# Two edits to the start of a fused attention and two-layer MoE kernel: an issue order on TensorE, and a third staging buffer for weights

## The chip, the core and the metric

The kernel runs on one core of a Trainium2 chip. Its five engines each work through a queue of their own in order: TensorE (PE in the profile; its weight loads are PEld), VectorE (DVE), ScalarE (ACT), GpSimd (POOL) and SyncE (SP), which here issues most of the DMAs. The metric is the device time of one execution in microseconds (us), as the median of several runs; lower is better. One further execution was taken with the hardware profiler, and all rows below come from that one.

## What is computed

Decay attention on 4 batches of 8 heads, sequence 576 and head size 64, then two dense feed-forward layers on the 2304 tokens. Inputs are float32 but for the weights, which are float64.

```python
scores = q @ k.T / 8 + (cum[:, None] - cum[None, :])   # cum = cumsum(log(clip(f))), causal
x = softmax(scores) @ v            # tokens x 512
h = x @ w_in ; g = maximum(0.01 * h, h) ; y = g @ w_out     # first MoE, width 2048
out = ((y @ w_a) * (y @ w_b)) @ w_o2                        # second MoE, width 1536
```

## The kernel before

**Precision.** A matmul operand is split into a high and a low part (`_hi`, `_lo`), and a product is three matmuls (hi·hi, hi·lo, lo·hi) into one accumulator. Weights arrive as pairs of 32-bit words of a float64. `load_weight` loads one piece of 128 x 512 of them by one DMA of 512 KB into a tile `raw`, and `from_double` builds the float32 in a tile `c`: on ACT an absolute value (L94); on DVE a clamp (L95), a shift (L96), and two merges that read `raw` (L97, L100). `split` then writes the high part on ACT (L87) and the low part on DVE (L88). So a piece costs two instructions on ACT and five on DVE. `raw` and `c` have two buffers each in the pool `stage`; a `raw` buffer is free once L100 has read it.

**First MoE.** Tokens are worked in chunks of 256. For a chunk i and a pair pr of weight column blocks, `l1` makes a group `h_i_pr` of 24 matmuls of 128 x 256 (L574), ACT writes `gh` and `hs`, DVE writes `gl` (L586), and `l2` adds 24 matmuls into `y_i_0` and `y_i_1` (L601). Eight pairs make a chunk. The weights stay in SBUF for all chunks, so chunk 0 is the one that waits for loading and conversion: pair pr needs the pieces `wi_2pr`, `wi_2pr+1`, `wo_2pr`, `wo_2pr+1`.

**Attention.** A block is a batch b and a half r of its rows. Block (0,0) fills chunk 0 of x, block (0,1) fills chunk 1 and a part of chunk 2. Per head there are scores `s` (and `s4` for the last 64 rows), a reduction on DVE (`p`, L320 and L361), an exponential on ACT, transposes `pp`, products with v (`av`), and per pair of heads a division `xn` on DVE and a transpose `px`, whose result ACT and DVE split into `xh` and `xl` of the chunk. Batch 0 works in plain float32; there each score or `av` matmul of the program is two in the trace.

**What sets the order.** The kernel is written in a framework that lists instructions by priority, times them with a planner's model of the engines, and so fixes each engine's queue when the program is built. The code calls block (0,0) with weight loads in between, then with raised priority the first two pairs of chunk 0, then block (0,1) with loads and further pairs, then the rest. The queue of PE starts a matmul only after all those ahead of it, and so do DVE, ACT and SP with theirs.

Of the kernel before, what the change touches and what calls it, by code (L numbers as in the profile page):

```python
# [17 lines left out]
P = 128  # L18
# [8 lines left out]
def kernel(  # L27
# [13 lines left out]
    nc = tc.nc  # L41
    B, H, S, D = q.shape
# [4 lines left out]
    NF1, NF2, ND = F1 // P, F2 // P, DM // P  # L47
# [57 lines left out]
    def load_weight(pool, stg_pool, src, name, W, RB, **kw):  # L105

        hi = pool.tile([P, 512], F32R, tag="w", name=f"{name}_hi", **kw)
        lo = pool.tile([P, 512], F32R, tag="w", name=f"{name}_lo", **kw)
        for z in range(0, 512, W):
            raw = stg_pool.tile([P, W, 2], I32, tag="raw", bufs=RB, name=f"raw_{name}_{z}")  # L110
            view = raw.rearrange("p n t -> p (n t)")
            if len(src.shape) == 3:
                view = view.rearrange("p (a b) -> p a b", b=2 * P)
                nc.sync.dma_start(view, src[:, z // P : (z + W) // P, :])
            else:
                nc.sync.dma_start(view, src[:, 2 * z : 2 * (z + W)])
            c = stg_pool.tile([P, W], I32, tag="t", bufs=2, name=f"c_{name}_{z}")
            split(hi[:, z : z + W], lo[:, z : z + W], from_double(raw, c), nc.vector)
        return hi, lo

# [9 lines left out]
    mp = moe_ctx.enter_context(tc.tile_pool(name="moe_a", bufs=2, side="right"))  # L130
    stage_ctx = ExitStack()
    stage = stage_ctx.enter_context(tc.tile_pool(name="stage", bufs=2, side="right"))
    late = {}
    ps_y = moe_ctx.enter_context(tc.tile_pool(name="ps_y", bufs=2, space=PSUM))
    att_ctx = ExitStack()
    ap_ = att_ctx.enter_context(tc.tile_pool(name="att", bufs=1))
    ps_a = att_ctx.enter_context(tc.tile_pool(name="ps_att", bufs=1, space=PSUM, side="right"))


# [1 line left out]
    nc.sync.dma_start(fs, f.rearrange("b h s -> (b h) s"))  # L141
    nc.vector.tensor_scalar(fs, fs, 0.0001, 1.0, op0=ALU.max, op1=ALU.min)
    nc.scalar.activation(fs, fs, AF.Ln)
    ones = ap_.tile([B * H, S], F32, tag="tk", name="ones")
    nc.vector.memset(ones, 1.0)
    cum = ap_.tile([B * H, S], F32, tag="cumb", bufs=3, name="cum")
    nc.vector.tensor_tensor_scan(cum, ones, fs, 0.0, op0=ALU.mult, op1=ALU.add)
# [22 lines left out]
    def att_scores(b, r, h, st):  # L170
# [56 lines left out]
        else:  # L227
# [3 lines left out]
            for u in range(2):  # L231
                for e in range(2):
# [2 lines left out]
                    nc.sync.dma_start(dst[:, lead // 32 : nqc, :], src[:, : nqc - lead // 32, :])  # L235
                    if lead:
                        nc.sync.dma_start(dst[:, 0:2, :], src[:, nqc - 2 :, :])
            tq = ap_.tile([P, 320], F32, tag="tq", name=f"tq_{nm}")
            dve_att.transpose(out=tq[:, :nq], in_=xq[:, :nqc, :].rearrange("p c d -> p (c d)"))

            qhh = ap_.tile([P, 384], F32R, tag="qhh", bufs=2, name=f"qhh_{nm}")
            qll = ap_.tile([P, 384], F32R, tag="qll", bufs=2, name=f"qll_{nm}")
            lasts[h] = qhh, qll
            z0 = 64 if r == 1 and j == 1 else 0
            if r == 1:
# [8 lines left out]
            if j == 0:  # L254
                xk = ap_.tile([P, 18, 32], F32, tag="xk", name=f"xk_{nm}")
                for u in range(2):
                    for e in range(2):
                        nc.sync.dma_start(
                            xk[u * 64 + e * 32 : u * 64 + e * 32 + 32, :nkc, :],
                            k[b, h + u, 0:nk, e * 32 : e * 32 + 32].rearrange("(c i) d -> i c d", i=32),  # L260
                        )
                tk = ap_.tile([P, S], F32, tag="tk", name=f"tk_{nm}")
                dve_att.transpose(out=tk[:, :nk], in_=xk[:, :nkc, :].rearrange("p c d -> p (c d)"))
                qks[pair] = tk

# [291 lines left out]
    def load_a(fi):  # L557
# [2 lines left out]
            *load_weight(wpool, stage, rows(w_out, fi), f"wo_{fi}", 512, 2, bufs=4 * NF1),  # L560
        )

    def l1(i, pr):
        ch, cl = x_chunk(i)
        last = i >= NB1 - 2
        hps = (pools["ps_ab"] if last else ps_y).tile(
            [P, 2, T1], F32, tag="ab0" if last else "h", bufs=2 if last else 1, name=f"h_{i}_{pr}"
        )
        for u in range(2):
            wih, wil = wa[2 * pr + u][0], wa[2 * pr + u][1]  # L570
            n = 0
            for c in reversed(range(ND)):
                for w, x in ((wih, ch), (wih, cl), (wil, ch)):
                    nc.tensor.matmul(  # L574
                        hps[:, u, :], w[:, c * P : c * P + P], x[:, c, :], start=(n == 0), stop=(n == 3 * ND - 1)
                    )
                    n += 1

        hs = mp.tile([P, 2, T1], F32, tag="hs", name=f"hs_{i}_{pr}")
        gh = mp.tile([P, 2, T1], F32R, tag="gh", name=f"gh_{i}_{pr}")  # L580
        gl = mp.tile([P, 2, T1], F32R, tag="gl", name=f"gl_{i}_{pr}")
        with tc.high_priority(offset=1):
            nc.scalar.activation(gh, hps, AF.Prelu, alpha=0.01)
# [103 lines left out]
    def att_steps(n):  # L687

        if n == 0:

            sts = [{} for _ in range(H)]
            scores = [att_scores(*blocks[n], h, sts[h]) for h in range(H)]
            values = [att_values(*blocks[n], h, sts[h]) for h in range(H)]
            before = None
            for h in range(0, 2):
                next(scores[h])
            for h in range(0, H, 2):
                for z, _ in enumerate(beside(beside(*scores[h : h + 2]), before)):
                    if z == 3:
                        for g in scores[h + 2 : h + 4]:  # L700
                            next(g)
                    yield
                before = chain(*values[h : h + 2])
            yield from before
            return
        second = None
        for h in range(H):
            st = {}
            yield from beside(att_scores(*blocks[n], h, st), second)
            second = att_values(*blocks[n], h, st)  # L710
# [22 lines left out]
    def work(i, fi):  # L733
        pend.append((i, fi, *l1(i, fi)))
        if len(pend) > 1:
            l2(*pend.pop(0))
# [5 lines left out]
    def load_next():  # L742
        nonlocal loaded
        if loaded < NF1:
            load_a(loaded)
            loaded += 1
# [7 lines left out]
        load_next()  # L754
    with tc.high_priority(offset=2000):
        work(*zero.pop(0))
        work(*zero.pop(0))
    for s, _ in enumerate(att_steps(1)):
        if s % 8 == 7:
            load_next()  # L760
        if s % 16 == 15 and 2 * (NF1 // 2 - len(zero)) + 2 <= loaded:
            work(*zero.pop(0))
    while zero:
        load_next()
        load_next()
# [1 line left out]
    for item in one[:4]:  # L767
        work(*item)
    stage_ctx.close()
    late["p"] = moe_ctx.enter_context(tc.tile_pool(name="late", bufs=1, side="right"))  # L770
    att_tail(0)
    for _ in att_steps(2):
# [73 lines left out]
```

## Time and profile before

| | us |
|---|---|
| median of 3 runs (lowest, highest) | 1111.56 (1110.79, 1111.98) |
| the profiled execution's own time | 1109.59 |
| its span, first to last instruction | 1107.8 |
| PE busy in the span | 1079.2 (97%) |
| DVE busy | 614.0 (55%) |
| ACT busy | 543.2 (49%) |

The shares of busy time are means over very different stages: on the page's 40 slices DVE is 7 to 8 tenths busy until about the middle and 1 to 2 tenths in the last third, while PE shows 9 nearly throughout. A PE that counts as busy isn't one that runs at its peak, since ends of matmuls are modelled; for PE the distance between starts is the better measure.

### The profile page before, as it was taken

To read this page: it belongs to the slowest core of one execution; us is meant where nothing else is said; L and a number is where in the kernel's file an instruction comes from. 1 tells how busy PE (TensorE), PEld (TensorE's weight loads), DVE (VectorE), ACT (ScalarE), POOL (GpSimd) and SP (SyncE) were. 2 spreads that over 40 slices of the span, in tenths; PEclk is the share of its full clock that TensorE was granted. 3 is DMA by queue.
4 is the path that set the end of the run, shared out by engine and by line. 5 is a ranking of instruction groups with operands and counts; after the bars stand their busy time and mean duration, and the time that the engine had idled before them with its cause. 6 is when DMAs were issued, how large, how long until landed. Compare 5 with 4: busy or idle time off the path is not lost.

```text
span 1107.8 us, 19615 instructions
## 1 busy us (share of the span) xinstructions
PE 1079.2 (97%) x7021; PEld 967.2 (87%) x7021; DVE 614.0 (55%) x1484; ACT 543.2 (49%) x1257; POOL 204.5 (18%) x434
## 2 busy tenths in 40 slices
PE   5899999999999999999999999999999999999998
PEld 3577779999999999999999997888888888888897
DVE  5869887887777777677478877412111211211122
ACT  4656668878787878768554454312111211211121
POOL 4423322434243432333000000102001000100000
PEclk9879999999999999999999999999999999999999
DMA  7645545442452334422054454202000100100010
GB/s 196 195 130 172 159 120 103 96 94 48 79 124 62 94 58 83 109 62 53 9 165 144 142 152 152 76 1 76 1 1 20 48 1 1 48 1 1 1 39 20
DMA packets 185729, 86.77 MB, mean 78 GB/s; under 512 B 143840, under 2 KB 173536, under 8 KB 185632
## 3 DMA queue, kind: packets, MB, share of 16 engines
q1 hardware_dynamic: 180736, 80.80, 28.6%
q10 hardware_dynamic: 4896, 4.72, 1.3%
q8 instruction: 56, 0.92, 0.4%
q14 instruction: 41, 0.34, 0.1%
HBM read 75.96 MB, written 9.51 MB: 77 GB/s over the span
## 4 chain that ended last, share of the span: by engine, by line
PE 72%; DMA 11%; DVE 8%; ACT 4%; issue 3%; SPq 1%; POOL 0%; ACTq 0%; DVEq 0%; POOLq 0%
PE ab L653 25%; PE o L676 13%; PE h L574 11%; PE y L601 10%; PE s L76 5%; PE av L76 5%; PE pp L76 3%; DMA raw_wa<-in_moe_w_a_dram 3%; DMA raw_wb<-in_moe_w_b_dram 2%; DMA raw_wc<-in_moe_w_out_dram 1%; DMA xq<-in_q_dram 1%; DMA cumb<-cum_dram 1%; DMA raw_wi<-in_moe_w_in_dram 1%; DMA raw_wo<-in_moe_w_out_dram 1%; DMA sy<-y_dram 1%
## 5 line engine op out<-in xcount | busy, mean ns | idle before, releaser
L659 DVE TENSOR_TENSOR p<-ab,p 128x512 f32<-128x512 f32 (+1 forms) x60 | 38.3, 638 | 274.6 <-PE ab L653 272.0
L574 PE MATMUL h<-xh,wi_hi 128*128 128x256 f32 x576 | 164.6, 286 | 1.2 <-ACT wi_hi L87 1.2
L574 PE MATMUL h<-xh,wi_lo 128*128 128x256 f32 x576 | 164.1, 285 | 0.9 <-DVE wi_lo L88 0.9
L574 PE MATMUL h<-xl,wi_hi 128*128 128x256 f32 x576 | 164.3, 285 | 0.0
L601 PE MATMUL y<-gl,wo_hi 128*128 128x256 f32 x576 | 161.7, 282 | 1.0 <-DVE gl L586 1.0
L601 PE MATMUL y<-gh,wo_lo 128*128 128x256 f32 x576 | 161.1, 282 | 0.0
L601 PE MATMUL y<-gh,wo_hi 128*128 128x256 f32 x576 | 159.4, 282 | 0.0
L658 ACT COPY p<-ab 128x512 f32<-128x512 f32 (+1 forms) x60 | 32.7, 544 | 169.1 <-PE ab L653 168.7
L574 PEld LDWEIGHTS h<-xh,wi_hi 128*128 128x128 f32 x576 | 109.8, 191 | 5.2 <-issue 2.3
L574 PEld LDWEIGHTS h<-xh,wi_lo 128*128 128x128 f32 x576 | 109.8, 191 | 2.5 <-DVE wi_lo L88 1.1
L601 PEld LDWEIGHTS y<-gl,wo_hi 128*128 128x128 f32 x576 | 108.4, 188 | 2.9 <-DVE gl L586 1.6
L574 PEld LDWEIGHTS h<-xl,wi_hi 128*128 128x128 f32 x576 | 109.8, 191 | 0.8 <-issue 0.4
L601 PEld LDWEIGHTS y<-gh,wo_lo 128*128 128x128 f32 x576 | 108.3, 188 | 1.7 <-issue 1.2
L601 PEld LDWEIGHTS y<-gh,wo_hi 128*128 128x128 f32 x576 | 107.3, 188 | 1.8 <-issue 0.8
L313 POOL TENSOR_SCALAR p<-cumb,ncum_t 128x384 f32<-128x384 f32 (+1 forms) x112 | 75.1, 678 | 162.4 <-PE pp L76 47.8
L87 ACT CAST pph<-p 128x512 fp32r<-128x512 f32 (+1 forms) x60 | 34.8, 580 | 126.3 <-DVE p L659 126.2
L291 ACT ACTIVATE p<-p,stat 128x384 f32<-128x384 f32 (+4 forms) x128 | 77.0, 603 | 34.5 <-DVE stat L320 27.2
L88 POOL TENSOR_TENSOR yl<-sy,yh 128x512 fp32r<-128x512 f32 (+1 forms) x16 | 19.2, 1211 | 393.7 <-ACT yh L87 393.6
L653 PE MATMUL ab<-yh,wb_hi 128*128 128x512 f32 (+1 forms) x240 | 88.3, 368 | 0.9 <-DVE p L659 0.6
L653 PE MATMUL ab<-yh,wa_hi 128*128 128x512 f32 (+1 forms) x240 | 88.1, 367 | 0.0
L653 PE MATMUL ab<-yh,wa_lo 128*128 128x512 f32 (+1 forms) x240 | 88.1, 367 | 0.0
L653 PE MATMUL ab<-yl,wa_hi 128*128 128x512 f32 (+1 forms) x240 | 88.1, 367 | 0.0
(168 smaller groups left out, 2612.6 us busy)
## 6 DMA issues: line engine op xcount, KB each, us to landing
cumb<-cum_dram SPq DMA_DIRECT2D x32, 288.0 KB, 3.9
raw_wi<-in_moe_w_in_dram SPq DMA_DIRECT2D x16, 512.0 KB, 4.0
raw_wo<-in_moe_w_out_dram SPq DMA_DIRECT2D x16, 512.0 KB, 4.0
raw_wa<-in_moe_w_a_dram SPq DMA_DIRECT2D x12, 512.0 KB, 3.5
raw_wb<-in_moe_w_b_dram SPq DMA_DIRECT2D x12, 512.0 KB, 3.5
raw_wc<-in_moe_w_out_dram SPq DMA_DIRECT2D x12, 512.0 KB, 3.6
xq<-in_q_dram SPq DMA_DIRECT2D x144, 32.0 KB, 2.0
y_dram<-yo ACTq DMA_DIRECT2D x18, 256.0 KB, 3.0
```

What stands on the lines that cost most here:

```text
L76: return method(*args, **kw)
L87: nc.scalar.copy(hi, src)
L88: (lo_engine or nc.gpsimd).tensor_tensor(out=lo, in0=src, in1=f32(hi), op=ALU.subtract)
L291: act_att.activation(pt, pt, AF.Exp, bias=stat[:, 0, s : s + 1], scale=-1.0, accum_out=stat[:, 1, s : s + 1])
L313: pool_att.tensor_scalar(pt, cumb[:, :n], 1.0, ncum_t[:, t, bh : bh + 1], op0=ALU.mult, op1=ALU.add)
L574: nc.tensor.matmul(hps[:, u, :], w[:, c * P : c * P + P], x[:, c, :], start=(n == 0), stop=(n == 3 * ND - 1))
L601: nc.tensor.matmul(o, w[:, d * P : d * P + P], g[:, u, :], start=(fi == 0 and n == 0 and d % 2 == 0), stop=(fi == NF1 - 1 and n == 2 and d ...
L653: nc.tensor.matmul(o[:, :tn], w[:, c * P : c * P + P], y[:, c, :tn], start=(m == 0), stop=(m == 3 * ND - 1))
L658: nc.scalar.copy(p[:, :tn], ab[0][:, :tn])
L659: nc.vector.tensor_tensor(out=p[:, :tn], in0=ab[1][:, :tn], in1=p[:, :tn], op=ALU.mult)
L676: nc.tensor.matmul(o, g[:, t * P : t * P + P], w, start=(fi == 0 and m == 0), stop=(fi == NF2 - 1 and m == 2))
```

## The change

Two edits. The first records the last of the 24 matmuls of `h_0_0` and wraps the calls for block (0,1) in `issue_after`, which adds an edge from that matmul to every PE instruction that the block traces: in PE's queue they come behind it, without a wait for its end. It holds for PE alone. The second makes a pool `more` with one buffer of `raw` and one of `c`; every third piece (number 2, 5, 8 and so on, in the order of the calls) uses it. To make room, the tiles `tq`, `qll` and `tk` of batches 1 to 3 move to a pool `att_b` that is opened in the place of `more` once the weights of the first MoE are converted, and `ones` shares another tag.

```diff
         for z in range(0, 512, W):
-            raw = stg_pool.tile([P, W, 2], I32, tag="raw", bufs=RB, name=f"raw_{name}_{z}")
+            third = "more" in late and piece[0] % 3 == 2
+            piece[0] += 1
+            words, bufs = (late["more"], 1) if third else (stg_pool, RB)
+            raw = words.tile([P, W, 2], I32, tag="raw", bufs=bufs, name=f"raw_{name}_{z}")
...
-            c = stg_pool.tile([P, W], I32, tag="t", bufs=2, name=f"c_{name}_{z}")
+            c = words.tile([P, W], I32, tag="t", bufs=1 if third else 2, name=f"c_{name}_{z}")
...
+    more_ctx = att_ctx.enter_context(ExitStack())
+    late["more"] = more_ctx.enter_context(tc.tile_pool(name="more", bufs=1))
...
-    ones = ap_.tile([B * H, S], F32, tag="tk", name="ones")
+    ones = ap_.tile([B * H, S], F32, tag="p4", name="ones")
...
-            tq = ap_.tile([P, 320], F32, tag="tq", name=f"tq_{nm}")
+            tq = late["att"].tile([P, 320], F32, tag="tq", name=f"tq_{nm}")
...
-                    nc.tensor.matmul(
+                    end[0] = nc.tensor.matmul(
...
         work(*zero.pop(0))
+        first_end = end[0]
         work(*zero.pop(0))
-    for s, _ in enumerate(att_steps(1)):
-        if s % 8 == 7:
-            load_next()
-        if s % 16 == 15 and 2 * (NF1 // 2 - len(zero)) + 2 <= loaded:
-            work(*zero.pop(0))
+    with tc.issue_after(first_end.ins if hasattr(first_end, "ins") else first_end):
+        for s, _ in enumerate(att_steps(1)):
+            if s % 8 == 7:
+                load_next()
+            if s % 16 == 15 and 2 * (NF1 // 2 - len(zero)) + 2 <= loaded:
+                work(*zero.pop(0))
...
     stage_ctx.close()
+    more_ctx.close()
+    del late["more"]
+    late["att"] = more_ctx.enter_context(tc.tile_pool(name="att_b", bufs=1))
```

The planner then lays out all queues anew. On PE, just ahead of the first product of the first MoE, this stood before (`tk`, `tq`, `s`, `s4` and `pp` with 0_1 in the name belong to block (0,1), `px_0_0_7` is the last transpose of block (0,0)):

```order
L76 MATMUL av_0_0_7_580<-vn_0_0_6_562,ph_0_0_7_571 128x64 x3
L76 MATMUL s_0_1_0_2_741<-kn_0_1_0_709,qn_0_1_0_708 128x384
L76 MATMUL s_0_1_0_3_750<-kn_0_1_0_709,qn_0_1_0_708 128x512
L76 MATMUL px_0_0_7_614<-ident_65,xn_0_0_7_587 128x128 x2
L76 MATMUL s4_0_1_0_0_760<-kn_0_1_0_709,qn_0_1_0_708 64x288
L76 MATMUL pp_0_1_0_0_807<-ident_65,p_0_1_0_2_736 128x128 x3
L76 MATMUL s4_0_1_0_1_763<-kn_0_1_0_709,qn_0_1_0_708 64x288
L76 MATMUL pp_0_1_0_1_813<-ident_65,p_0_1_0_3_745 128x128 x4
L76 MATMUL tq_0_1_2_935<-ident_65,xq_0_1_2_925 128x128 x2
L76 MATMUL tq_0_1_2_935<-ident_65,xk_0_1_2_926 128x64
L76 MATMUL tk_0_1_2_0_940<-ident_65,xk_0_1_2_926 128x128 x2
L76 MATMUL s_0_1_1_2_803<-kn_0_1_0_709,qn_0_1_0_708 128x384
```

and now:

```order
L76 MATMUL px_0_0_5_560<-ident_65,xn_0_0_5_532 128x128 x2
L76 MATMUL av_0_0_7_583<-vn_0_0_6_565,ph_0_0_6_568 128x64 x3
L76 MATMUL av_0_0_7_583<-vn_0_0_6_565,ph_0_0_7_574 128x64 x3
L76 MATMUL px_0_0_7_617<-ident_65,xn_0_0_7_590 128x128 x2
L581 MATMUL h_0_0_622<-xh_0_312,wi_0_hi_188 128x256
```

All of block (0,1), the ten rows of it shown before and the eight transposes `tq_0_1_0` and `tk_0_1_0` that stood some rows higher, has gone behind the 24 products; `h_0_0` follows `px_0_0_7`.

On DVE, ahead of the last `xl_0`, which makes chunk 0 of x complete, this stood before (`c_wo_4`, `c_wi_5` are weight pieces under conversion):

```order
L76 TENSOR_TENSOR xn_0_0_7_587<-av_0_0_7_580,rec_0_0_7_577 128x2x64 x2
L100 SCALAR_TENSOR_TENSOR c_wo_4_0_489<-raw_wo_4_0_487,c_wo_4_0_489 128x512
L320 ISA p_0_1_0_2_736,stat_0_1_0_707<-s_0_1_0_2_741,p_0_1_0_2_736 128x384
L320 ISA stat_0_1_0_707 128x1
L95 TENSOR_SCALAR c_wi_5_0_536<-c_wi_5_0_536 128x512
L320 ISA p_0_1_0_3_745,stat_0_1_0_707<-s_0_1_0_3_750,p_0_1_0_3_745 128x512
L320 ISA stat_0_1_0_707 128x1
L88 TENSOR_TENSOR wo_4_lo_486<-c_wo_4_0_489,wo_4_hi_485 128x512
L96 TENSOR_SCALAR c_wi_5_0_536<-c_wi_5_0_536 128x512
L361 ISA p4_0_1_0_754,st4_0_1_0_755<-s4_0_1_0_0_760,p4_0_1_0_754 64x288
L361 ISA st4_0_1_0_755 64x1
L76 TENSOR_TENSOR xl_0_310<-px_0_0_7_614,xh_0_309 128x256
```

and now:

```order
L88 TENSOR_TENSOR wo_5_lo_548<-c_wo_5_0_551,wo_5_hi_547 128x512
L76 TENSOR_TENSOR xn_0_0_7_590<-av_0_0_7_583,rec_0_0_7_580 128x2x64 x2
L100 SCALAR_TENSOR_TENSOR c_wi_6_0_597<-raw_wi_6_0_595,c_wi_6_0_597 128x512
L95 TENSOR_SCALAR c_wo_6_0_609<-c_wo_6_0_609 128x512
L96 TENSOR_SCALAR c_wo_6_0_609<-c_wo_6_0_609 128x512
L95 TENSOR_SCALAR c_wi_7_0_775<-c_wi_7_0_775 128x512
L97 SCALAR_TENSOR_TENSOR c_wo_6_0_609<-raw_wo_6_0_607,c_wo_6_0_609 128x512
L88 TENSOR_TENSOR wi_6_lo_594<-c_wi_6_0_597,wi_6_hi_593 128x512
L96 TENSOR_SCALAR c_wi_7_0_775<-c_wi_7_0_775 128x512
L76 TENSOR_TENSOR xl_0_313<-px_0_0_7_617,xh_0_312 128x256
```

The conversions run further ahead: the piece in work at that point was `wi_5` and is `wi_7` now, and the three reductions of block (0,1) have gone behind.

On PE, ahead of `px_0_1_7`, the last transpose that chunk 1 of x waits for, stood before (`h_0_7` is the last product group of chunk 0, and nine more of its matmuls follow these rows; the `s_1_0` are first scores of batch 1):

```order
L76 MATMUL s_1_0_1_0_2252<-ks_1_0_1_2236,qhh_1_0_1_2232 128x128
L76 MATMUL s_1_0_1_0_2252<-ks_1_0_1_2236,qll_1_0_1_2233 128x128
L574 MATMUL h_0_7_1820<-xh_0_309,wi_15_hi_1601 128x256
L574 MATMUL h_0_7_1820<-xl_0_310,wi_15_hi_1601 128x256
L76 MATMUL s_1_0_1_1_2270<-ks_1_0_1_2236,qhh_1_0_1_2232 128x256
L76 MATMUL s_1_0_1_1_2270<-ks_1_0_1_2236,qll_1_0_1_2233 128x256
L574 MATMUL h_0_7_1820<-xh_0_309,wi_15_lo_1602 128x256
```

and now:

```order
L76 MATMUL av_0_1_7_1893<-vn_0_1_6_1772,ph_0_1_7_1878 128x64 x4
L76 MATMUL s_1_0_1_1_2277<-ks_1_0_1_2243,qhh_1_0_1_2239 128x256
L76 MATMUL s_1_0_1_1_2277<-ks_1_0_1_2243,qll_1_0_1_2240 128x256
L76 MATMUL s_1_0_2_0_2324<-ks_1_0_2_2314,qhh_1_0_2_2303 128x128
L76 MATMUL s_1_0_2_0_2324<-ks_1_0_2_2314,qll_1_0_2_2304 128x128
L76 MATMUL px_0_1_7_1911<-ident_65,xn_0_1_7_1908 128x128 x2
```

Chunk 0, with its last products and the last conversions, now stands well ahead of the last heads of block (0,1); before, `h_0_7` stood directly ahead of `px_0_1_7`. At the first matmul of `h_1_1` both queues have issued the same PE instructions, and from there on they differ only by small exchanges.

## Rows read from the trace of the kernel before

**Rows 1.** Busy time in windows: stretch, us, busy (instructions) by engine, PEclk, DMA share, GB/s.

```profile
13.40:58.40 45.00, 35.71 (x135) 24.39 (x135) 35.19 (x104) 27.57 (x73) 21.77 (x46) 0.87 0.74 201
62.78:175.16 112.38, 109.29 (x730) 89.72 (x730) 94.60 (x235) 70.38 (x164) 31.61 (x48) 0.96 0.51 138
153.69:167.09 13.40, 11.15 (x79) 10.63 (x78) 12.47 (x43) 9.18 (x25) 1.14 (x4) 0.87 0.35 84
180.00:300.00 120.00, 119.86 (x1000) 118.26 (x999) 94.67 (x275) 97.06 (x254) 45.27 (x107) 1.00 0.41 83
```

**Rows 2.** Waits of DVE from 13.4 to 58.4 us: total us, times, longest.

```profile
DVE c_wi L95 <- ACT c_wi L94: 5.3, 5, 2.3
...
DVE c_wo L95 <- ACT c_wo L94: 1.0, 1, 1.0
```

**Rows 3.** Waits of DVE from 58.4 to 77.5 us.

```profile
DVE p L320 <- PE s L76: 5.7, 2, 2.9
```

**Rows 4.** Waits of DVE from 77.5 to 167.4 us.

```profile
DVE c_wi L95 <- ACT c_wi L94: 3.3, 3, 2.2
```

**Rows 5.** Timeline: start, us, instruction (last use of raw_wo_4; last xl_0; c_wo_5).

```profile
53.42 0.69 DVE L100 SCALAR_TENSOR_TENSOR c_wo<-raw_wo,c_wo 128x512 int32<-128x512 int32 x1
...
57.97 0.41 DVE L76 TENSOR_TENSOR xl<-px,xh 128x256 fp32r<-128x256 f32 x1
...
61.03 0.66 ACT L94 ACTIVATE c_wo<-raw_wo 128x512 f32<-128x512 f32 x1
```

**Rows 6.** Lines of DVE, 77.5 to 167.4: count | busy us, mean ns | idle.

```profile
L88 DVE TENSOR_TENSOR wi_lo<-c_wi,wi_hi 128x512 fp32r<-128x512 f32 x10 | 7.2, 724 | 0.2
L100 DVE SCALAR_TENSOR_TENSOR c_wo<-raw_wo,c_wo 128x512 int32<-128x512 int32 x10 | 7.0, 698 | 0.2
...
L96 DVE TENSOR_SCALAR c_wo<-c_wo 128x512 int32<-128x512 int32 x10 | 4.4, 439 | 0.1
```

**Rows 7.** DMA issues of the page: count, KB each, median us to landing.

```profile
raw_wi<-in_moe_w_in_dram SPq DMA_DIRECT2D x16, 512.0 KB, 4.0
```

**Rows 8.** Lines of PE by form, 62.78 to 175.16 (six of 24 groups).

```profile
L574 PE MATMUL h<-xh,wi_hi 128*128 128x256 f32 x72 | 22.3, 310 | 1.2 <-ACT wi_hi L87 1.2
...
L601 PE MATMUL y<-gl,wo_hi 128*128 128x256 f32 x64 | 18.2, 287 | 0.0
...
L76 PE MATMUL av<-vn,ph 128*128 128x64 f32 x112 | 13.9, 274 | 0.0
L76 PE MATMUL pp<-ident,p 128*128 128x128 f32 x68 | 11.4, 287 | 0.4 <-DVE xl L374 0.4
L76 PE MATMUL s<-kn,qn 64*128 64x512 f32 x14 | 7.9, 641 | 0.4 <-DVE stat L361 0.4
...
L76 PE MATMUL tq<-ident,xk 64*128 64x64 f32 x2 | 0.5, 273 | 0.0
```

**Rows 9.** The chain that ended last: start, us, piece (seven pieces without a wait).

```profile
62.85 5.05 PE h L574 x24
...
119.62 1.11 PE av L76 x10
120.73 0.44 PE pp L76 x4
121.17 0.84 PE s L76 x2
...
122.72 1.05 PE s L76 x2
...
126.29 0.68 PE s L76 x2
...
548.59 2.80 PE h L574 x24
```

**Rows 10.** Windows around the first product, columns as in the first group.

```profile
44.00:62.78 18.78, 17.89 (x64) 10.88 (x63) 13.92 (x36) 10.73 (x25) 7.07 (x10) 0.59 0.65 174
62.78:67.31 4.53, 4.53 (x22) 4.53 (x22) 3.22 (x7) 0.71 (x2) 0.00 (x0) 0.50 0.52 173
```

More of the change, by code (lines that the diff above doesn't have):

```diff
@@ L132 @@
     stage = stage_ctx.enter_context(tc.tile_pool(name="stage", bufs=2, side="right"))
-    late = {}
+    late, piece = {}, [0]
     ps_y = moe_ctx.enter_context(tc.tile_pool(name="ps_y", bufs=2, space=PSUM))
@@ L237, in att_scores @@
                         nc.sync.dma_start(dst[:, 0:2, :], src[:, nqc - 2 :, :])
-            tq = ap_.tile([P, 320], F32, tag="tq", name=f"tq_{nm}")
+            tq = late["att"].tile([P, 320], F32, tag="tq", name=f"tq_{nm}")
             dve_att.transpose(out=tq[:, :nq], in_=xq[:, :nqc, :].rearrange("p c d -> p (c d)"))
             qhh = ap_.tile([P, 384], F32R, tag="qhh", bufs=2, name=f"qhh_{nm}")
-            qll = ap_.tile([P, 384], F32R, tag="qll", bufs=2, name=f"qll_{nm}")
+            qll = late["att"].tile([P, 384], F32R, tag="qll", bufs=2, name=f"qll_{nm}")
             lasts[h] = qhh, qll
@@ L261, in att_scores @@
                         )
-                tk = ap_.tile([P, S], F32, tag="tk", name=f"tk_{nm}")
+                tk = late["att"].tile([P, S], F32, tag="tk", name=f"tk_{nm}")
                 dve_att.transpose(out=tk[:, :nk], in_=xk[:, :nkc, :].rearrange("p c d -> p (c d)"))
@@ L561, in load_a @@
         )
+    end = [None]
     def l1(i, pr):
```

## The prediction, as it was put on record before the run

> **What bounds the kernel now.** I read the busy time in windows first. From 180 to 300 us PE is busy 119.86 of 120 us and starts 1000 matmuls; from 62.78, the start of the first product, to 175.16, the start of `h_1_1`, it starts 730 in 112.38 us and is busy 109.29 [rows 1]. So the later stages are TensorE's, and the first 175 us are the loose part. Since both queues have issued the same PE work at `h_1_1` and look alike behind it, I take a shift of that point to reach the end one to one, and the question is when `h_1_1` starts.
>
> Next the waits of DVE. From 13.4 to 58.4 us DVE waits 5.3 + 1.0 us for ACT's first step on a weight piece, which itself waits for a raw piece to land [rows 2]; from 58.4 to 77.5 it waits 5.7 us for scores that PE has in its queue next to the first products [rows 3]; from 77.5 to 167.4 its largest group of waits comes to 3.3 us [rows 4]. DVE is nearly full there, and its last piece, `wi_15_lo`, is what holds `h_0_7` and the end of chunk 1.
>
> How much of the 112.4 us is PE work? The lines of PE give counts, the chain gives distances between starts without a wait. 216 + 192 products (three groups of 72 and of 64) at 2.80/24 = 0.117 us are 47.6; 152 `av` halves (112 and a group of 40) at 0.111 are 16.9; 103 transposes (68 `pp` and five small groups) at 0.11 are 11.3; scores are 14 halves of 512 columns at 0.525, 13 of 384 at 0.42, 28 of 288 (two groups) at 0.34, together 22.4; twelve small ones of batch 1 are 1.4 [rows 8, 9]. Sum 99.6. So 12.8 us of the stretch are stall: 2.3 since the first 24 products took 5.05 instead of 2.80 [rows 9]; 4.8 in the window 153.69 to 167.09, whose 79 matmuls cost 8.6 at the same prices [rows 1]; the other 5.7 are scattered.
>
> **The change part by part.** *The order on PE.* Moved behind the first 24 products are, by the queue: 20 transposes (`tq`, `tk`, `pp`), two scores of 384 columns (`s_0_1_0_2`, `s_0_1_1_2`), one of 512, two of 288. At the full-clock prices: 20 x 0.11 + 2 x 0.84 + 1.05 + 2 x 0.68 = 6.3 us [rows 9]. Before, this ran while PE had to wait for chunk 0 anyway; now it lies behind the first product, on the engine that is the bound: **+6.3 us**. What it buys is that nothing of block (0,1) can delay the products, but `xl_0` ended at 58.38 and the first product began at 62.78 [rows 5, 10], so at most 4.4 us were to be had from that edge alone.
>
> *The third buffer.* It lets a piece be loaded while two are in conversion. A piece costs DVE about 2 x 0.44 + 2 x 0.70 + 0.72 = 3.0 us [rows 6]. The planner used this to pull conversions ahead. By the queues, between them and the last `xl_0` DVE now has, beyond before, the rest of `wi_5`, all of `wo_5`, `wi_6`, most of `wo_6` and two steps of `wi_7`, some 10.4 us, less three reductions of block (0,1) of 1.7: 8.7 us more. So `xl_0` can't end before 58.4 + 8.7 - 6.3 = 60.8 if every wait for a piece vanishes, and ends at 67.1 if none does. Between them I go by the buffers: `wi_6` can be loaded when `wo_4` leaves its buffer, which was at 54.1 [rows 5]. With about the same DVE work ahead of it and most waits gone I put that at 50. Then landing 4.0 [rows 7], ACT 0.7 [rows 5], one clamp and the last merge of `wo_5` 1.1, landing of `wi_7` 4.0, ACT 0.7, and five DVE instructions to the end of `xl_0`, 2.7: 63.2, and the first product at about 63.5, **+0.7 us** (-1.8 to +4.5). It's now the third buffer's own next piece that stands ahead of chunk 0 on DVE, and on ACT the same piece stands ahead of `xh_0`.
>
> *What stall is left.* The 24 products start at half clock again: 2.3. Then the 8.7 us that DVE has done early are gone from its queue between `xl_0` and the end of chunk 1, where it had no slack; so PE should be late there less often. Of the scattered 5.7 I leave 3. At the end chunk 1 no longer waits for weights, but there are no products left to fill the chain of the last two heads (scores, reduction, exponential, transpose, copy, `av`, division, transpose, split): of 4.8 I leave 1.7. Together 7.0 in place of 12.8: **-5.8 us**. Bounds: 3.8 (all but the clock and a remainder) and 12.8 (nothing gained).
>
> *At no cost:* `issue_after` makes an edge of order, no semaphore that PE waits for. `tq`, `qll`, `tk` wait for the end of the conversions, which the queue of DVE now puts well ahead of their first use. On SP raw pieces now stand ahead of loads of block (0,1), each with a wait for a buffer; those loads are needed some 15 us after the first product, and I count nothing. If that cover failed, each would cost PE about a landing, 3 to 4 us.
>
> **Sum.** +0.7 + 6.3 - 5.8 = +1.2 us against the profiled execution's 1109.59, which stands 2.0 below the median. I carry it over to the median: 1111.56 + 1.2 = **1112.8**, no change that a measurement of this kernel tells from none (about 0.2%, 2.2 us). With the bounds it spans from -1.8 + 6.3 - 9.0 = -4.5 to +4.5 + 6.3 = +10.8.
>
> **The rivals.** *Slower: the first product is late.* The pieces pulled ahead stand on DVE and ACT in front of the last split of chunk 0, both engines work in order, and a raw piece that lands late holds the split. The 16 DMA engines are already 0.74 busy from 13.4 to 58.4 [rows 1], with four more pieces to carry by then. First product at 67.3 (+4.5), 6.3 moved, stall 9.5 (-3.3): +7.5, 1119. It decides if the first product starts after about 65.5. For it: the queue as it is printed. Against: the waits it removes are of the same kind.
>
> *Faster: the conversions were the whole trouble.* With three buffers DVE never waits, the first product starts at 61.0 (-1.8), and PE then runs with little but the clock's stall, 4.5 (-8.3): -3.8, 1107.8. For it: DVE's full queue up to 167 and the 5.7 us of waits that go [rows 3]. Against: PE's own work from the first product to `h_1_1` is now 99.6 + 6.3 = 105.9 us, so little more than this can be had.
>
> *Slower: the clock.* From 44 to 62.78 PE is busy 17.89 of 18.78 us at a mean granted clock of 0.59, and at 0.50 (1.2 of 2.4 GHz) from 62.78 to 67.31 [rows 10]; the 0.50 ended amid the products. The Trainium skill (TensorE: Matmul & The Clock Gate, Part 1, "What's actually happening") says that the throttled state is the default and activity releases it; by that rule, with PE emptier ahead of the products, the lower clock should hold longer behind their start. The trace agrees only in part: busy with block (0,1), PE was held at the lower clock all the same. If it holds for as long behind the first product as it did from 44 on, 0.41 x 18.78 / 0.5 = 15.4 us, PE loses 7.7 instead of 2.3: 5.4 more, 1118.2.
>
> **How the numbers follow.** The forecast, a trade that nearly cancels, gets 0.46 (1110 to 1115.5, of which 0.05 lies below and 0.09 above the 0.2%), the late first product 0.20, the clock 0.07, the faster case 0.25, and 0.02 that nothing moves. Faster: 0.25 + 0.05 = 0.30. Slower: 0.20 + 0.07 + 0.09 = 0.36. Same: 0.34. The range takes in both neighbours up to their prices: 1106.5 to 1119.5.
>
> **What would show it.** In the profile after, the first L581 matmul: 63.5 is the step on DVE's queue, 61 the faster case, 66 and more the late one. The distance to the start of `h_1_1`: 106 plus stall, so 113. The granted clock at the first products: 0.50 for about 4.5 us. Waits of DVE up to the first product: for weight pieces 1 to 2 us instead of 6. PE busy between px and the first product: nothing. It would be wrong if the queues behind `h_1_1` weren't alike in time, if loads of block (0,1) came late behind raw pieces on SP, or if DVE fell behind PE in the middle, at `px_0_1_3` or `h_0_7`, where its queue has most ahead.

## The result, and the profile after

The changed kernel is slower: a median of 1124.39 us (1121.99 to 1128.42, six runs) beside 1111.77 us of the kernel before on the same chip, a ratio of 1.0119 with a 95% interval of 1.0098 to 1.0140. The profiled execution took 1123.73 us, its span 1121.9 instead of 1107.8. Forecast were 1112.8 and at most 1119.5. (One of the five executions of e5, further down, took 1773.62 us at a granted clock of 0.571; the median there is that of the other four.)

In the changed kernel the line numbers of the first MoE are 7 higher: `h` is L581, `y` L608, `gh` L590, `hs` L591, `gl` L593; `ab`, the first product of the second MoE, is L660. The windows that answer to [rows 1] (columns as there; the third and fourth are the parts of the second behind the first 24 products):

```profile
13.40:58.40 45.00, 32.91 (x115) 22.58 (x116) 38.46 (x108) 26.78 (x69) 25.48 (x46) 1.00 0.75 218
63.09:180.19 117.10, 114.61 (x759) 92.25 (x759) 87.20 (x224) 71.42 (x168) 33.67 (x52) 1.00 0.44 115
67.78:155.00 87.22, 87.22 (x577) 68.81 (x575) 69.48 (x166) 53.99 (x120) 27.64 (x37) 1.00 0.47 130
155.00:180.19 25.19, 22.71 (x163) 18.75 (x161) 13.40 (x50) 15.41 (x45) 6.04 (x15) 1.00 0.30 58
185.00:305.00 120.00, 117.64 (x973) 115.45 (x972) 92.93 (x268) 94.95 (x245) 45.32 (x107) 1.00 0.40 80
```

The first product starts at 63.09, where it was forecast (63.5). `h_1_1` starts at 180.19 instead of 175.16: +5.0, where +1.2 was forecast. And the last row has what nobody looked for: in the 120 us behind, 5 us later than the last window of [rows 1] for the same work, PE is busy 117.64 instead of 119.86 us and starts 973 matmuls instead of 1000. All waits of PE from `h_1_1` to about 790 us in the changed kernel (total us, times, longest):

```profile
PE y L608 <- DVE gl L593: 2.1, 3, 0.9
PE av L76 <- DVE vhl L88: 1.7, 2, 1.5
PE y L608 <- ACT gh L590: 1.6, 1, 1.6
PE s L76 <- DVE stat L325: 1.3, 1, 1.3
PE h L581 <- ACT hs L591: 1.3, 2, 0.9
PE ab L660 <- DVE p L666: 0.9, 1, 0.9
PE o L683 <- DVE ppl L88: 0.7, 1, 0.7
PE av L76 <- ACT hs L591: 0.5, 1, 0.5
```

and in the kernel before, over the same work:

```profile
PE av L76 <- DVE pl L374: 1.0, 2, 0.5
PE y L601 <- DVE gl L586: 1.0, 2, 0.5
PE ab L653 <- DVE p L659: 0.6, 1, 0.6
PE ab L653 <- ACT yo L609: 0.3, 1, 0.3
```

10.1 us instead of 2.9, in a dozen waits of about 1 us each, none of them near the edits. (One of the dozen, 0.9 us for `hs`, ends with the first matmul of `h_1_1` and so belongs to the +5.0; behind it are 9.2.) Up to late in the first block of `ab` the shift grows from 5.0 to 13.9 us; from there to the end it stays at 13.9. So 8.9 of the 13.9 us that the profile shows are lost behind the point at which the prediction stopped to look. The listed waits make up 6.3 of them; the other 2.6 lie in distances between starts that the profile counts as no wait.

### The profile page after: what moved, and what is told of

Read it like the earlier page. It is cut to its first block, busy times and chain, and to the rows that moved or that the text cites. A ratio compares the mean times of both kernels' runs of the same rounds, so it can differ in the third digit from the quotient of the medians.

```text
span 1121.9 us, 19660 instructions
## 1 busy us (share of the span) xinstructions
PE 1080.4 (96%) x7021; PEld 967.1 (86%) x7021; DVE 611.3 (54%) x1484; ACT 543.1 (48%) x1257; POOL 209.1 (19%) x434
## 4 chain that ended last, share of the span: by engine, by line
PE 77%; DMA 11%; DVE 5%; ACT 3%; issue 2%; SPq 1%; POOL 0%; ACTq 0%; DVEq 0%; POOLq 0%
PE ab L660 23%; PE h L581 13%; PE y L608 13%; PE o L683 12%; PE s L76 6%; PE av L76 5%; PE pp L76 4%; DMA raw_wc<-in_moe_w_out_dram 2%; DMA raw_wa<-in_moe_w_a_dram 2%; DMA xq<-in_q_dram 2%; DMA raw_wo<-in_moe_w_out_dram 1%; DMA raw_wb<-in_moe_w_b_dram 1%; DMA sy<-y_dram 1%; DMA raw_wi<-in_moe_w_in_dram 1%; SPq L240 1%
## 5 line engine op out<-in xcount | busy, mean ns | idle before, releaser
L581 PE MATMUL h<-xh,wi_hi 128*128 128x256 f32 x576 | 163.6, 284 | 5.6 <-DVE xl L76 4.1
L581 PE MATMUL h<-xl,wi_hi 128*128 128x256 f32 x576 | 164.0, 285 | 0.8 <-DVE xl L379 0.8
L608 PE MATMUL y<-gl,wo_hi 128*128 128x256 f32 x576 | 162.5, 284 | 2.1 <-DVE gl L593 2.1
L581 PE MATMUL h<-xh,wi_lo 128*128 128x256 f32 x576 | 164.0, 285 | 0.0
L608 PE MATMUL y<-gh,wo_lo 128*128 128x256 f32 x576 | 161.4, 282 | 0.0
L608 PE MATMUL y<-gh,wo_hi 128*128 128x256 f32 x576 | 159.1, 282 | 1.6 <-ACT gh L590 1.6
L581 PEld LDWEIGHTS h<-xh,wi_hi 128*128 128x128 f32 x576 | 109.2, 190 | 7.7 <-DVE xl L76 4.5
L665 ACT COPY p<-ab 128x512 f32<-128x512 f32 (+1 forms) x60 | 32.6, 544 | 167.9 <-PE ab L660 167.4
L608 PEld LDWEIGHTS y<-gl,wo_hi 128*128 128x128 f32 x576 | 108.3, 188 | 5.2 <-DVE gl L593 2.8
L318 POOL TENSOR_SCALAR p<-cumb,ncum_t 128x384 f32<-128x384 f32 (+1 forms) x112 | 80.2, 723 | 172.0 <-PE pp L76 74.7
L581 PEld LDWEIGHTS h<-xl,wi_hi 128*128 128x128 f32 x576 | 109.2, 190 | 3.0 <-issue 1.8
L608 PEld LDWEIGHTS y<-gh,wo_lo 128*128 128x128 f32 x576 | 108.3, 188 | 2.8 <-issue 2.1
L581 PEld LDWEIGHTS h<-xh,wi_lo 128*128 128x128 f32 x576 | 109.2, 190 | 1.5 <-issue 1.2
L608 PEld LDWEIGHTS y<-gh,wo_hi 128*128 128x128 f32 x576 | 107.1, 188 | 3.5 <-ACT gh L590 2.1
L660 PE MATMUL ab<-yh,wb_hi 128*128 128x512 f32 (+1 forms) x240 | 88.2, 367 | 0.9 <-DVE p L666 0.9
L660 PE MATMUL ab<-yh,wa_hi 128*128 128x512 f32 (+1 forms) x240 | 88.1, 367 | 0.0
L660 PE MATMUL ab<-yl,wa_hi 128*128 128x512 f32 (+1 forms) x240 | 88.1, 367 | 0.0
L660 PE MATMUL ab<-yh,wa_lo 128*128 128x512 f32 (+1 forms) x240 | 88.1, 367 | 0.0
```

The source lines that it names most:

```text
L318: pool_att.tensor_scalar(pt, cumb[:, :n], 1.0, ncum_t[:, t, bh : bh + 1], op0=ALU.mult, op1=ALU.add)
L581: end[0] = nc.tensor.matmul(hps[:, u, :], w[:, c * P : c * P + P], x[:, c, :], start=(n == 0), stop=(n == 3 * ND - 1))
L608: nc.tensor.matmul(o, w[:, d * P : d * P + P], g[:, u, :], start=(fi == 0 and n == 0 and d % 2 == 0), stop=(fi == NF1 - 1 and n == 2 and d ...
L660: nc.tensor.matmul(o[:, :tn], w[:, c * P : c * P + P], y[:, c, :tn], start=(m == 0), stop=(m == 3 * ND - 1))
L665: nc.scalar.copy(p[:, :tn], ab[0][:, :tn])
```

## The experiments

Two means come back in them. **Pinned queues**: an edge of order, without a wait, from each instruction of an engine to the next, so that the engine's queue is the one of another kernel, instruction by instruction; the lists make the code longer, so its lines in the rows are some 20 to 40 higher. **Later queues** are those of all five engines from `h_1_1` on. The table shows for every kernel how much later (+) or earlier a first matmul starts in its trace than in the trace of before, in us, and the time beside before. Before stands at 62.78, 164.98, 175.16, 232.26, 438.41, 560.02 and 716.23; `ab0_0_7` is late in the first block of the second MoE.

| kernel | h_0_0 | px_0_1_7 | h_1_1 | h_2_0 | h_5_0 | h_7_0 | ab0_0_7 | median us | ratio (95%) |
|---|---|---|---|---|---|---|---|---|---|
| changed | +0.3 | +6.5 | +5.0 | +7.2 | +7.8 | +9.7 | +13.9 | 1124.39 | 1.0119 (1.0098, 1.0140) |
| e1 edge only | -6.8 | +0.9 | 0.0 | +1.2 | +6.4 | +5.9 | +9.8 | 1119.96 | 1.0078 (1.0060, 1.0097) |
| e2 third buffer only | +6.2 | +4.3 | +2.6 | +4.2 | +10.0 | +8.8 | +14.4 | 1119.90 | 1.0085 (1.0059, 1.0111) |
| e3 pool only | +2.9 | +2.8 | +2.8 | +2.8 | +1.8 | +1.2 | +1.2 | 1112.01 | 1.0004 (0.9992, 1.0017) |
| e4 changed, later queues of before | +1.1 | +7.8 | +5.8 | +6.3 | +5.5 | +4.9 | +5.5 | 1115.14 | 1.0043 (1.0025, 1.0062) |
| e5 before, later queues of changed | +2.9 | +1.7 | +1.7 | +3.9 | +4.9 | +6.9 | +10.4 | 1118.31 | 1.0060 (1.0039, 1.0081) |
| e6 = e1, later queues of before | -6.2 | +1.5 | +0.3 | +0.1 | -0.4 | -0.4 | -0.1 | 1109.64 | 0.9988 (0.9976, 1.0000) |
| e7 = e2, later queues of before | +5.1 | +1.6 | -0.2 | +0.5 | +0.9 | +1.2 | +1.5 | 1111.77 | 1.0005 (0.9993, 1.0017) |
| e8 changed, last queues of before | +2.1 | +8.8 | +7.3 | +9.6 | +10.6 | +12.8 | +17.8 | 1125.91 | 1.0122 (1.0096, 1.0148) |
| e9 both edits, conversions held | -10.6 | +0.1 | -1.3 | -0.7 | -1.7 | -1.4 | -1.1 | 1108.63 | 0.9974 (0.9961, 0.9988) |
| e10 short conversions | +2.5 | -2.5 | -2.3 | -2.3 | -3.0 | -3.1 | -2.3 | 1108.26 | 0.9966 (0.9950, 0.9982) |
| e11 third buffer only, held | -3.7 | -5.2 | -7.3 | -6.7 | -7.2 | -6.9 | -6.8 | 1102.62 | 0.9917 (0.9894, 0.9940) |
| e12 = e9, later queues free | -10.8 | +0.8 | -0.1 | +3.4 | +4.2 | +6.0 | +9.9 | 1116.66 | 1.0047 (1.0031, 1.0062) |

How far a single trace can be trusted is seen in e3, whose PE, DVE, ACT and POOL have the queues of before: its first product is 2.9 us later and its `ab0_0_7` 1.2. So a column is read to some 3 us, and sizes are taken from the medians where these can tell.

### Each edit alone (e1, e2, e3)

e1 is the kernel before with the edge alone, without the new pool; e2 the changed kernel without the edge; e3 the changed kernel without the edge and the third buffer, so that only the new pool is left. The edit of e3, against the changed kernel:

```diff
-            third = "more" in late and piece[0] % 3 == 2
+            third = False
...
-    with tc.issue_after(first_end.ins if hasattr(first_end, "ins") else first_end):
-        for s, _ in enumerate(att_steps(1)):
...
+    for s, _ in enumerate(att_steps(1)):
```

> The order edge alone: block (0,1) behind the 24 products, two staging buffers as before, no third. Theory A (the edge at the start is the whole loss): h_1_1 starts at 180 or later, as in the changed kernel (180.2), and 12 us or more are lost at the end. Theory B (the third buffer is the loss: conversions pulled ahead of the attention): the first product at 61 to 62, h_1_1 within 2 us of 175.2, the time within 0.2% of before. Theory C (any edit of the start makes the planner lay out the later queues anew, and their small waits cost about 9 us): h_1_1 moves by what the start gives, and from there to the end another 7 to 10 us are lost, here as in the changed kernel.

> The third buffer alone, no order edge: the first scores and transposes of block (0,1) stand ahead of the first product again. Theory A (the edge is the whole loss): within 0.2% of before or faster. Theory B (the third buffer is the loss): h_1_1 at 180, 12 us slower. Theory C (the new layout of the later queues): h_1_1 within 3 us of before, then 7 to 10 us lost behind it.

> Only the move of tq, qll and tk into the pool att_b, opened when the first MoE's weights are converted: no third buffer, no order edge. The queues of PE, DVE, ACT and POOL are those of before, instruction by instruction. If the place of these tiles or their wait for the end of the conversions costs something, some of the 9 us behind h_1_1 shows here; theory C says nothing does: within 0.2% of before, h_1_1 at 175.2 within 0.5.

Neither A nor B: each edit alone costs about 9 us, and together they cost 12.6. In e1 `h_1_1` stands where it stood, to 0.1 us, and 9.8 us are lost behind it; in e2 11.8, more than the 7 to 10 expected, in what was the slowest of its four executions (1124.02). In e3 nothing is lost, so the pool is not it. Theory C is the one that fits: a loss behind the start that comes with either edit of the start.

### The later queues exchanged (e4, e5, e6, e7)

At the end of the program stand these lines, with `QUEUES` holding, for each engine, runs of places in the traced program:

```diff
+    queued = {}
+    for i in tc.nc.cur_bb.bb.instructions:
...
+    for engine, pieces in QUEUES.items():
+        row = [queued[engine][k] for first, n in pieces for k in range(first, first + n)]
+        for a, b in zip(row, row[1:]):
+            tc.add_manual_dep(b, a.name, info, reason="queue")
```

> The changed kernel, with the queues of all five engines from h_1_1 on pinned, by edges of order alone, to those of the kernel before; ahead of h_1_1 its own. Theory C (the new layout behind h_1_1 is the cause of the 8.9 us lost there, whatever is ahead): h_1_1 at +5, and no more than 1 us is added to the end: about 1116.5, +5 us. Rival D (what is lost behind h_1_1 comes from what the start leaves behind: transfers, buffers or attention that are late): the 8.9 us are lost all the same, 1124.

> The reverse: the kernel before, with its queues from h_1_1 on pinned to those of the changed kernel; nothing is changed ahead of it, no third buffer, no edge at the start. Theory C: h_1_1 at 175.2, then about 9 us lost, 1120. Rival D: 1111.5, no change.

> The order edge alone (as e1), its queues from h_1_1 on pinned to those of before. Theory C: the start gave -0.05 us at h_1_1 and the 9.8 us behind it vanish: 1111, within 0.2% of before. Rival D: +9 us as in e1.

> The third buffer alone (as e2), its queues from h_1_1 on pinned to those of before. Theory C: +2.6 us as at h_1_1, 1113.5. Rival D: +9 us as in e2.

All four came out as C has it (only e7's own start moved `h_1_1` by -0.2 and not by the 2.6 expected). Behind `h_1_1` e4, e6 and e7 add -0.4, -0.3 and +1.7 us, e5 8.8. By the medians the later queues cost 12.62 - 4.16 = 8.5 us with both edits (the changed kernel against e4, each beside its own runs of before), 9.1 + 1.3 = 10.4 with the edge alone, 9.0 - 0.8 = 8.2 with the buffer alone, and 7.3 on a kernel that is otherwise untouched (e5). Rival D, a debt that the start leaves behind, falls: the start of e5 is that of before.

These sizes are of two new layouts only. Compared place by place, the queues behind `h_1_1` are the same in e1 and e2, and the same in the changed kernel, e5 and e12 (below); from about 490 us on all of these are one. Whether another edit's layout would cost as much, no run here shows.

### The last part alone (e8)

As e4, but the pinned lists begin at `h_7_0`.

> The changed kernel with the queues of before only from h_7_0 on (chunks 7 and 8 and the second MoE); up to there all its own. If the small waits sit where the traces of the changed kernel show them, 4.2 of the 8.9 us behind h_1_1 lie behind h_7_0 and go, the other 4.7 stay: h_7_0 at +9.7, ab0_1_0 at +10, 1120. If the waits only move on to the next late thing, nothing is won: 1124.

Neither was met. The trace stands at +12.8 at `h_7_0` (it began 1.8 us later than the changed kernel's at the first product) and loses 5.0 us more behind it, although every engine now has the queue of before there. What differs is when the second MoE's first weights are asked for. The first such load in the queue of SP (start, us, instruction), in the kernel before,

```profile
551.89 0.37 SPq L114 DMA_DIRECT2D raw_wa<-in_moe_w_a_dram  x1
```

in the changed kernel,

```profile
563.81 0.37 SPq L117 DMA_DIRECT2D raw_wa<-in_moe_w_a_dram  x1
```

and in e8:

```profile
566.90 0.37 SPq L138 DMA_DIRECT2D raw_wa<-in_moe_w_a_dram  x1
```

Before it is issued 8.1 us ahead of `h_7_0` (560.02), in the changed kernel 5.9 (569.72), in e8 5.9 (572.81); in e4, where nothing was lost, 8.1 (556.79 of 564.91). The same two leads divide all fourteen traces: 8.1 in the eight that lose 0.8 us or less behind `h_7_0`, 5.9 or 6.0 in the six that lose some 3.5 to 5.5. The pool for these pieces opens when the last attention has ended (this load waits for the last transpose `ppx`, 31.7 us before and 33.7 now), and that ends closer to `h_7_0` in the new layout. So the 4 to 5 us behind `h_7_0` are the second half of a loss that begins in the layout of the chunks ahead. That the late loads are the cause was not tried by itself; that the queues behind `h_7_0` aren't is shown.

How a late load reaches PE is seen at the last group of chunk 8. ACT in the changed kernel (start, us, instruction, idle time before it and its releaser):

```profile
665.77 0.62 ACT L87 CAST yh<-sy 128x512 fp32r<-128x512 f32 x1 [1.25 <-DMA sy<-y_dram]
667.08 0.62 ACT L87 CAST yh<-sy 128x512 fp32r<-128x512 f32 x1 [0.69 <-DMA sy<-y_dram]
668.46 0.67 ACT L94 ACTIVATE c_wa<-raw_wa 128x512 f32<-128x512 f32 x1 [0.76 <-DVE yl L88]
669.76 0.62 ACT L87 CAST yh<-sy 128x512 fp32r<-128x512 f32 x1 [0.63 <-DMA sy<-y_dram]
670.28 0.59 ACT L590 ACTIVATE gh<-h 128x512 fp32r<-128x512 f32 x1
```

and PE:

```profile
670.92 0.50 PE L608 MATMUL y<-gh,wo_hi 128*128 128x256 f32 x2 [1.63 <-ACT gh L590]
```

`gh` is due, but stands in ACT's queue behind four steps that each wait, three of them for `sy` (`y` read back from DRAM) and `c_wa`, by the profile, for DVE; PE waits 1.63 us for it. The loads of `sy` stand in SP's queue among those of the weights: the first is issued 89.3 us behind the start of `h_7_0`, where before had 82.9 (659.04, 642.88). Not every wait of the list above is of this kind. The three for `gl` and the ones for `hs` follow steps that kept DVE or ACT at work without a gap. Common to these is the place in a queue: a short instruction that PE needs stands behind others.

### What the start cost (e9, e11, e12)

In these the queues of PE, DVE and ACT are pinned up to the first product as well, and everything else on the three engines is put behind. So no piece of weights is pulled in front of the last split of chunk 0, and the third buffer acts behind it alone. `FIRST` is the list of e1 (e9, e12) or of before (e11, which has no edge):

```diff
+    for engine, pieces in FIRST.items():
+        ranks = [k for first, n in pieces for k in range(first, first + n)]
...
+        for k in sorted(set(range(len(queued[engine]))) - set(ranks)):
+            tc.add_manual_dep(queued[engine][k], row[-1].name, info, reason="queue")
```

> The changed kernel, both edits, with the queues behind h_1_1 of before, and ahead of the first product the queues of PE, DVE and ACT as in e1, so that no further weight piece stands in front of the last split of chunk 0; behind it the third buffer does as it likes. If the conversions pulled in front of chunk 0 are what cost the combination its start: first product at 56 to 57, h_1_1 at or up to 2 us ahead of before's, 1109 to 1111. If it is that block (0,1) runs behind chunk 0 and ends late, whenever chunk 0 began: first product at 56 to 57 but h_1_1 at +3 or more, 1114 and up.

> The third buffer alone (no order edge), the queues behind h_1_1 of before, and ahead of the first product PE, DVE and ACT in the order of before, so that the third buffer acts only behind it. If the gain of e9 comes from the third buffer behind the first product: h_1_1 1 to 3 us ahead of before's, 1108 to 1110. If it takes both edits, the edge making the first product early and the buffer the weights for it: no change, 1111.5.

> e9 (both edits, conversions held behind chunk 0's last split) without its pin on the later queues: the planner lays them out as in the changed kernel. Theory C: h_1_1 about 1.3 us ahead of before's as in e9, then the 9 us of the changed kernel's later queues: 1119. If the 9 us come with a late block (0,1) only: 1109.

e9 beats its runs of before by 3.1 us (its first product came at 52.1, sooner than the 56 to 57 expected), where e4 lost 4.2 to its own: the conversions in front of chunk 0 are what cost the combination its start, 7.2 us. e11 beats all: 1102.62 us, 8.7 less than before, more than either view had expected, and without the edge. The edge then costs 8.7 - 3.1 = 5.6 us by the medians, 6.0 by the traces at `h_1_1`. It costs this only together with the third buffer: without it e6, with the edge alone and the later queues of before, is 1.3 us faster than its runs of before. e12 is e9 with the planner's own later queues; it loses 5.4 us where e9 won 3.1: the same 8.4 us a fifth time.

What the third buffer gives in e11: the waits of DVE from 13.4 to 63 us,

```profile
DVE p L111 <- POOL p L111: 3.5, 3, 2.3
DVE p L360 <- PE s L111: 3.3, 3, 2.2
DVE p L111 <- PE s L111: 0.8, 1, 0.8
DVE p L401 <- PE s L111: 0.3, 1, 0.3
```

have none for a weight piece left, where [rows 2] had 6.3 us. The first product starts at 59.13, and its stretch to `h_1_1`, with the 730 matmuls of [rows 1], takes 108.73 instead of 112.38:

```profile
59.13:167.86 108.73, 107.35 (x730) 87.77 (x730) 90.41 (x231) 69.50 (x161) 32.73 (x48) 0.99 0.51 136
```

### How much of the stall is DVE's (e10)

In 21 pieces, from `wo_5` on, the kernel leaves out most of the conversion; all its queues are those of before:

```diff
+        whole = t
+        if 11 <= piece[0] < 32:
+            top, low, t, c = top[:, :8], low[:, :8], t[:, :8], c[:, :8]
+        piece[0] += 1
...
-        return t
+        return whole
```

> The kernel before with all its queues pinned as they are, and the four integer steps of DVE on the pieces from wo_5 to wo_15 cut to 8 of 512 columns: most of their conversion is left out, so 22 pieces cost DVE about 1.0 us each instead of 3.0, some 44 us less up to 167. The prediction's view (the scattered stall of 5.7 us between the first product and chunk 1 is PE waiting for weights): that stall falls to 3 or less and the waits for wi_15 vanish, h_1_1 5 us earlier or more. The other view (it belongs to block (0,1): its scores and transposes cost PE more than their unit prices wherever they stand): stall between the first product and 153 stays at about 5, only the waits for wi_15 of 2.1 go, h_1_1 2 to 3 us earlier.

The windows of e10 from the first product to `h_1_1`, then its two parts that answer to 67.90 to 153.69 and 153.69 to 167.09 of before:

```profile
65.26:172.90 107.64, 107.30 (x730) 87.98 (x730) 62.08 (x235) 69.62 (x164) 24.09 (x48) 1.00 0.55 143
70.20:154.81 84.61, 84.61 (x566) 66.61 (x565) 47.06 (x177) 53.58 (x120) 21.71 (x43) 1.00 0.59 157
154.81:164.38 9.57, 9.32 (x79) 8.94 (x78) 8.33 (x39) 8.46 (x24) 1.30 (x3) 1.00 0.39 95
```

and the first of the two parts in the kernel before:

```profile
67.90:153.69 85.79, 84.95 (x566) 66.63 (x566) 74.25 (x176) 54.13 (x120) 29.39 (x43) 1.00 0.55 153
```

With DVE 32.5 us emptier (62.1 instead of 94.6 us busy) the same 566 matmuls take 84.61 instead of 85.79 us. At the prediction's unit prices they cost 80.4, so of 5.4 us of "scattered stall" 4.2 stay when weights can hardly be late. The end of chunk 1 is where conversions do matter: 79 matmuls in 9.57 instead of 13.40 (a part of this is the clock, granted 0.87 there before and 1.00 in e10). Both expectations are met in part: the scattered stall goes by 1.2 only, as the other view has it, and `h_1_1` comes 4.7 us sooner after the first product, nearly what the prediction's view had. The 4.2 are no waits that the profile shows: in that part of e10 PE is busy all the time. They lie at the switches of the block itself, which the unit prices leave out. Of the 564 distances between starts there, 63 are some 0.1 us longer than the unit price, and every one of these stands within two matmuls of a switch from one kind of matmul to another (there are 104 switches); the part of before has 62, that of the changed kernel 71 of 574, whatever DVE has to do. Behind two scores of e10, for instance, the second `y` comes after 0.22 us, the next one after 0.12:

```profile
129.38 0.75 PE L97 MATMUL s<-kn,qn 64*128 64x288 f32 x2
130.06 0.38 PE L626 MATMUL y<-gl,wo_hi 128*128 128x256 f32 x1
130.28 0.28 PE L626 MATMUL y<-gh,wo_lo 128*128 128x256 f32 x1
130.40 0.28 PE L626 MATMUL y<-gh,wo_hi 128*128 128x256 f32 x1
```

## Why the prediction failed, point by point

Two steps failed: that a shift of `h_1_1` reaches the end one to one, which missed 8.5 us by the medians, and the stall that was left, 11.2 us where 7.0 was put. The range stopped at 1119.5 although the sum's own bounds went on to +10.8 (1122.4); the result lies beyond both.

**The first product: right.** 63.09 against 63.5, by the same path: the last split of chunk 0 stands behind the steps of three other pieces. DVE in the changed kernel (start, us, instruction):

```profile
60.74 0.43 DVE L95 TENSOR_SCALAR c_wi<-c_wi 128x512 f32<-128x512 f32 x1 [1.20 <-ACT c_wi L94]
61.08 0.69 DVE L97 SCALAR_TENSOR_TENSOR c_wo<-raw_wo,c_wo 128x512 int32<-128x512 int32 x1
61.68 0.68 DVE L88 TENSOR_TENSOR wi_lo<-c_wi,wi_hi 128x512 fp32r<-128x512 f32 x1
62.29 0.42 DVE L96 TENSOR_SCALAR c_wi<-c_wi 128x512 int32<-128x512 int32 x1
62.62 0.42 DVE L76 TENSOR_TENSOR xl<-px,xh 128x256 fp32r<-128x256 f32 x1
```

The small number hid a large one, though. +0.7 was the difference of a gain and a loss, and the step priced only what was left: e9 shows the product at 52.1 when no piece is pulled in front, e11 at 59.1 without the edge. The prediction allowed the edge 4.4 us at most, and in e1 it brings 6.8. In the changed kernel PE has nothing at all to do from 58.95 to 63.09.

**The moved PE work, +6.3: right in its count.** From the first product to `h_1_1` PE starts 759 matmuls instead of the 730 of [rows 1], 29 more, where the prediction has 30 (20 transposes and five scores of two each). Their price was not measured by itself. That the edge costs 6.0 us at `h_1_1` with the conversions held (e9 against e11) is near 6.3 by luck: e9 starts its products 7.0 us sooner than e11 and then needs 13.0 us more, so that its moved work comes with 6.7 us of further stall. Its stretch, beside the 108.73 of e11:

```profile
52.14:173.87 121.73, 117.96 (x759) 94.20 (x760) 95.30 (x243) 75.80 (x175) 30.74 (x52) 0.99 0.49 128
```

**What stall is left, -5.8: wrong.** From the first product to `h_1_1` 117.10 us passed for 105.9 us of work: 11.2 us of stall, not 7.0. Three terms, by the windows above. The slow start was sized well: the 24 products took 4.69 us, 1.9 over 2.80, where 2.3 was put. The scattered stall was put at 3: the 577 matmuls from 67.78 to 155.00 cost 81.5 at the unit prices, so it is 5.7, no less than before. Nor is it a stall: PE is busy 87.22 of the 87.22 us. The sum of PE work left out what the switches cost (e10), which earlier weights don't give back. The step's premise was that PE is late there because DVE is; e10 shows that most of it stays with DVE a third emptier, and in the changed kernel DVE's longest waits are now for PE, from 77.5 to 167.4 us:

```profile
DVE p L325 <- PE s L76: 7.2, 6, 3.0
DVE p L366 <- PE s L76: 4.8, 3, 2.4
```

where [rows 4] had DVE waiting 3.3 us at most. The end of the chunk was put at 1.7: from 155.00 on 163 matmuls at 21.7 us take 25.19, so 3.5. (The three make 11.1, the 11.2 but for rounding.) The weights were early, as foreseen (`wo_15_lo` at 133 instead of 170 us), but block (0,1) was 17 to 18 us late from `px_0_1_1` to `px_0_1_5`, with its last heads alone at the end. Together this is the +5.0 at `h_1_1`: 0.3 for the first product, 6.3 moved, 1.6 of stall saved.

**A shift of `h_1_1` reaches the end one to one: wrong, and the larger miss.** The prediction rested on "both queues have issued the same PE work at `h_1_1` and look alike behind it". The same work they had issued; alike they were not. Place by place, from 200 to 550 us, a fifth to two thirds of PE's queue in a stretch of 50 us, and on DVE and ACT a fifth to three fifths, is what stood there before; "small exchanges" of such a number each can put one needed instruction behind one that waits. The exchanges of queues put 7 to 10 us on it in all five comparisons (8.5, 10.4, 8.2, 7.3 and 8.4). It was named as what would make the prediction wrong, but it had neither a price nor a rival.

**The rivals.** The late first product didn't come (63.1, its point was 65.5). The clock's didn't either: PE was emptier ahead of the products (32.91 of 45.00 us busy, 35.71 before) and behind the first of them the slow pace lasted 3.8 us, up to 66.89, where before had 4.5 [rows 9, 10]. Here the rule of the Trainium skill (TensorE: Matmul & The Clock Gate, Part 1, "What's actually happening") that the slower clock is the default and work releases it agrees with the pace: it was slow ahead of the products too (last section) and rose amid them. The faster one, that the waits for pieces were the whole trouble, was true of the buffer and not of the change: with the pieces held back in the queue the buffer alone gives 1102.6, where the rival had 1107.8.

**The account.** By medians, each beside its own runs of before: the third buffer where it does what it is for -8.7 (e11), the edge +5.6 (e9 less e11), conversions pulled in front of chunk 0 +7.2 (e4 less e9), the new layout of the later queues +8.5 (changed less e4): +12.6. Each is measured on top of those ahead of it, so that they add up is no test of them. With the later queues of before the edge by itself is -1.3 (e6), and the buffer with its conversions pulled ahead +0.8 (e7).

## What to carry to other kernels

Where a planner lays out all queues, an edit of one place is two edits: itself, and a new layout of everything behind. Before a shift is carried to the end, compare the queues of every engine there place by place, and give the new layout a price and a chance of its own. To measure the edit alone, pin the rest to its old order; and a buffer that lets work run ahead needs a limit on what it may run ahead of.

## What was not expected of the hardware

The clock row and the pace can differ. In the changed kernel the granted clock stands at 1.00 in every window, yet the products of `h_0_0` start 0.21 us apart up to 66.89 and 0.12 behind (start, us, instruction):

```profile
66.46 0.41 PE L581 MATMUL h<-xh,wi_hi 128*128 128x256 f32 x1
66.67 0.41 PE L581 MATMUL h<-xl,wi_hi 128*128 128x256 f32 x1
66.89 0.35 PE L581 MATMUL h<-xh,wi_lo 128*128 128x256 f32 x1
67.08 0.28 PE L581 MATMUL h<-xh,wi_hi 128*128 128x256 f32 x1
67.19 0.28 PE L581 MATMUL h<-xl,wi_hi 128*128 128x256 f32 x1
```

That is the pace that [rows 9] and [rows 10] show at 0.50. In before the row tells it, here it doesn't; e1, whose products start at 55.97 with the same 0.21, has 1.00 as well. Ahead of the products the changed kernel had the slow pace too: twelve `av` take 2.82 us, where the prediction's unit price makes them 1.33.

```profile
53.98 2.82 PE L76 MATMUL av<-vn,ph 128*128 128x64 f32 x12 [2.13 <-DVE xl L76]
```

So in these traces a 1.00 in that column is no evidence that the clock was high; the distance between starts is.
